# A delta-rule kernel followed by a mixer: the first loads in one queue, betas earlier, the first weight converted in the order of its use, and a new order of all instructions

## The chip, the cores and the metric

The kernel runs on one core of a Trainium2 chip. The metric is device time in microseconds (us), lower is better. A core has five engines that run their own instruction streams in order: TensorE (PE, with its weight loads shown as PEld), VectorE (DVE), ScalarE (ACT), GpSimd (POOL) and SyncE (SP), which here only issues transfers. Transfers move in DMA queues between HBM and the core's SBUF.

## The reference

Two computations stand one behind the other. For batch 4, 8 heads, 768 steps and head size 48:

```python
k_n = k / (norm(k) + 1e-06)
for t in range(S):
    y[t] = q[t] @ state
    v_old = state.T @ k_n[t]
    state = state + beta[t] * outer(k_n[t], v[t] - v_old)
```

The outputs of the 8 heads, side by side, are x (4, 768, 384). Then

```python
h = (x.T @ U @ V)          # over the sequence, rank 32
u = x + h.T
out = u + relu(u @ w_ch1) @ w_ch2    # 384 -> 1536 -> 384
```

U, V, w_ch1 and w_ch2 arrive as float64; all else is float32, and so are the matmuls.

## The kernel before, in words

**Units.** The delta rule is computed in chunks of 64 steps. A unit is one batch and one half of the sequence (6 chunks, all 8 heads), so there are 8 units; units 0 and 1 are batch 0. Two SBUF tiles (slot0, slot1) hold the units in turn, so unit 2 can be loaded when unit 0 is done. For each unit:

- `load` brings k, q, v and z (z is a second copy of half of k for the state update) in pieces of 72 KB. `load_beta` brings the betas and turns them with TensorE (L343), ScalarE (L350) and VectorE (L358).
- `grams` transposes k or q (L408 on PE, copied by L418/L420/L423), then multiplies k by k or k by q (L435). L445 and L448 cut the diagonal blocks out of the k products.
- `blocks` lays these blocks out (L517), scales them with the norms and betas (`norms`, L374 to L388, and L521) and inverts the small triangular blocks by substitution on VectorE (L526, L532, in 15 steps for units 0 and 1). The result is turned back (L539, L548).
- `joins` merges inverted blocks into larger ones with many small matmuls (L582, L596, L622 to L643), and `prepare` multiplies k and v by the inverse (L741, L752).
- `recur` steps over the chunks: b (L790), z on VectorE (L803), the state's update (L818, then L828 or L830 on VectorE), and the output in two parts (L705, L719), copied into X by ScalarE (L689).

**Mixer.** When a batch's 12 chunks are in X, `front` computes X @ U (L969), the correction with V (L983), adds it (L987), and transposes X for the products (L991, L994). `wide` does, for each third of a batch (i = 0, 1, 2): the first product (L1062, 12 blocks f of 128 columns, three matmuls each, ReLU by L1018 in pairs of blocks), then the second product in seven parts (L1099), which saves one multiplication of eight by sums of operands (S1, S2 and sums of w_ch2). A part works on 6 matmuls and is added to X by L1047; finished rows go out.

**Weights.** `load_weights` brings 14 slices of float64 (U, V, six of w_ch1, six of w_ch2) into three staging places (half of X, `wide`, part of `hs`) and rebuilds float32 from the bits: five VectorE instructions (L918, L924, L930, L936, L946) and one on ScalarE (L903) for each slice. Four sums for each half of w_ch2 (L858) follow. A slice of w_ch1 held 128 rows by half of the columns, so the first block of the first product needed three slices.

**What sets the order.** Each of these pieces is a Python generator that yields what it needs (`need(...)`) and what it is about to issue (`op(engine, cost, ...)`). `run` plays them against a model of the engines' clocks and each time issues the instruction that the model finds earliest, with the rank of the piece (second argument of `begin`, low first) as the tie-breaker. The emission order is then the order on every engine and queue, with no runtime choice: the costs, the ranks and the table of constants do nothing on the chip but set this order. TensorE's cost is multiplied by `state["slow"]` (1.9) until the first product starts. `lot`, `words` and `FETCH` model the fetching of TensorE's instructions.

Of the kernel before, what the change touches and what calls it, by code (L numbers as in the profile page):

```python
# [26 lines left out]
def kernel(  # L27
# [33 lines left out]
    NU = 2  # L61
# [23 lines left out]
    state = dict(now=0.0, mode=None, hw=0.0, slow=1.9, lot=63, fetched=0.0)  # L85
    free = dict(pair={x: 0.0 for x in range(4)}, mix={})
    done, parts, waits, ready, last = {}, {}, {}, {}, {}
    LAT = dict(pe=0.22, dve=0.06, act=0.06, pool=0.1, sp=0.0)
    SWITCH, HOLD = 0.18, 0.18
    LOT, FETCH = 256, 3.9  # L90

# [6 lines left out]
    def op(engine, cost, mode=None, take=None, give=(), lat=None, rush=None, words=0, port=None):  # L98
        return dict(
            e=engine, cost=cost, mode=mode, take=take, give=give, words=words + 2,  # L100
            port=engine == "pool" if port is None else port,
            rush=bool(give) if rush is None else rush, lat=LAT[engine] if lat is None else lat,
        )
# [4 lines left out]
    def emitted(key, after=0.0):  # L108
        done[key] = state["now"] + after

    def landing(packets, each=0.015):
        state["hw"] = max(state["hw"], state["now"]) + packets * each / 16
        return max(2.0, state["hw"] + 2.4 - state["now"])

    def advance(i, value, at):
        try:
            waits[i], ready[i] = parts[i].send(value), at
        except StopIteration:
            del waits[i]

    def begin(part, place):
        i = (place, len(parts))
        parts[i], waits[i] = part, []
        advance(i, None, state["now"])
# [5 lines left out]
    def cost_of(s):  # L130
        return s["cost"] * (state["slow"] if s["mode"] else 1.0)

# [8 lines left out]
    def run():  # L141
        stall = {}
        while waits:
            some = {}
            for i in sorted(waits):
                while isinstance(waits.get(i), list) and all(x in done for x in waits[i]):
                    at = max([0.0] + [done[x] for x in waits[i]])
                    if at > ready[i]:
                        last[i] = None
                    advance(i, None, max(at, ready[i]))  # L150
                s = waits.get(i)
                if s is None or isinstance(s, list):
                    continue
# [12 lines left out]
                some.setdefault(e, []).append((at + stall[i], i))  # L166
            if not some:
                continue
            picks = []
            for e, them in some.items():  # L170
                soon = min(at for at, _ in them)
                them.sort(key=lambda x: (not waits[x[1]]["rush"], x[1]))
                for at, i in them:
                    hold = 0.7 if i[0] < 13 else HOLD if i[0] < 90 else SWITCH
# [12 lines left out]
            cost = cost_of(s)  # L187
            if s["e"] == "pe":
                crossed, more = late(s, at)
                state["lot"] += s["words"]  # L190
                if state["lot"] > LOT:
                    state["lot"] -= LOT
                    cost += more
                    state["fetched"] = crossed + more + FETCH
# [79 lines left out]
    w1_sb = const.tile([128, KT, DFF], FP32, name="w1_sb")  # L274
# [9 lines left out]
    SPLIT, QUARTERED = (0, 1), (2,)  # L284

# [8 lines left out]
    def load(n, name, halves):  # L294
# [12 lines left out]
        queue = dict(sp=nc.sync, act=nc.scalar, pool=nc.gpsimd)[e]  # L307
# [17 lines left out]
    def load_beta(u):  # L325
# [10 lines left out]
        for cu in range(UC):  # L336
            c = UC * u + cu
            if cu % 3 == 0:
                got = yield op("pe", 0.4, "Q", take=None if cu else "pair", words=24)
            if cu == 0:  # L340
                x, p_bt = got, one(got)[:, 0 : 4 * B * UC].rearrange("p (c x) -> p c x", c=UC)
            for g in range(2):
                nc.tensor.matmul(  # L343
                    p_bt[half(g), cu], beta_sb[:, g, c * L : c * L + L],
                    ident[0 : 4 * B, 0 : 4 * B], start=True, stop=True,
                )
# [54 lines left out]
    def grams(n, i):  # L401
        kn, kq, pg, qk, qn, _, diag, _ = units[n]

        def turn(t, j, i):
            x = yield op("pe", 0.8, "F", take="pair", words=12)
# [22 lines left out]
        def products(j, i):  # L428
            yield need(("laid", n)) if i else []
            x = yield op("pe", 0.7, "Q", take="pair", words=96)  # L430
# [63 lines left out]
    def blocks(n):  # L494
# [66 lines left out]
        def joins(h):  # L561
# [5 lines left out]
            if split == 2:  # L567
# [6 lines left out]
                for y, e in enumerate(es):  # L574
                    if y % 6 == 0:
                        got = yield op("pe", 0.37, mode, take=None if y else "pair", words=words)
# [12 lines left out]
                for y, e in enumerate(es):  # L589
                    if y % 6 == 0:  # L590
                        got = yield op("pe", 0.37, mode, take=None if y else "pair", words=words)
# [23 lines left out]
            for y, (r, c) in enumerate(spots):  # L615
                if y % 3 == 0:
                    got = yield op("pe", 0.18, "J", take=None if y else "pair", words=48)
# [13 lines left out]
            for y, (r, c) in enumerate(spots):  # L631
                if y % 3 == 0:
                    got = yield op("pe", 0.18, "J", take=None if y else "pair", words=48)
# [43 lines left out]
    def recur(b):  # L677
# [19 lines left out]
        def outputs(c, s_old):  # L697
# [3 lines left out]
            y = yield op("pe", 0.24, "Q", take="pair", words=32)  # L701
            p_y = pair(y)[:, :, 0 : 2 * D]
            if c > 0:
# [11 lines left out]
                yield op("pe", 0.24, "Q", words=32)  # L715
# [16 lines left out]
        def prepare(n, h):  # L732
# [4 lines left out]
            x = yield op("pe", 0.7, "Q", take="pair", words=96)  # L737
# [10 lines left out]
            y = yield op("pe", 0.7, "Q", take="pair", words=96)  # L748
# [27 lines left out]
        for c in range(NC):  # L776
# [9 lines left out]
            else:  # L786
                xb = yield op("pe", 0.24, "Q", take="pair", words=32)
# [24 lines left out]
            if c < NC - 1:  # L812
                yield need(("y1", b, c)) if c else []
                xs = yield op("pe", 0.24, "Q", take="pair", words=32)
# [18 lines left out]
    WIDE = 768  # L833

    def weight_slices():
        yield u_sb.rearrange("p c r -> p (c r)"), moe_U, "c"
        yield v_sb, moe_V, ""
        for f in range(2):
            for t in range(KT):
                rows = slice(t * 128, t * 128 + 128)  # L840
                yield (
                    w1_sb[:, t].rearrange("p (a b x) -> p b a x", a=2, b=2)[:, f],
                    moe_w_ch1[rows].rearrange("p (a b x) -> p b a x", a=2, b=2)[:, f], "a",
                )
# [16 lines left out]
    def load_weights():  # L861
# [14 lines left out]
        def start(i):  # L876
# [9 lines left out]
            elif kind == "a":  # L886
                pieces = [(to.rearrange("p (a x) -> p a x", a=2), src)]
# [12 lines left out]
        def raised(i, power):  # L900
            cost = 0.16 + power.shape[1] * 0.001
# [9 lines left out]
        for i in range(len(slices)):  # L911
# [31 lines left out]
            if len(dst.shape) > 2:  # L943
                dst = dst if len(dst.shape) == 3 else dst.rearrange("p a f d -> p a (f d)")
# [14 lines left out]
    def front(b, i):  # L959
# [20 lines left out]
        def block(c):  # L980
# [7 lines left out]
            o = yield op("pe", 0.56, "F", take="pair", words=6)  # L988
# [20 lines left out]
    def wide(b, i):  # L1009
        yield need(("front", b, i), ("narrow", *before(b, i)))  # L1010
        x, ut = X[:, b % 2], uts[b, i]
        if b == 0 and i == 0:
            yield ["mixing"]
            state["slow"] = 1.0
# [40 lines left out]
        for y, fs in enumerate(((0, 1), (2, 6), (7, 8), (3, 4), (5, 9), (10, 11))):  # L1055
            for f in fs:
                yield need(("weights", 1 + KT * (f // 3 % 2 + 1)))
# [3 lines left out]
                for t in range(KT):  # L1061
                    nc.tensor.matmul(  # L1062
                        p_f[:, fs.index(f)],
                        w1_sb[:, t, f * 128 : (f + 1) * 128],
# [42 lines left out]
    with tc.manual_schedule():  # L1107
        begin(load(0, "k", (0,)), 3)
        begin(load(0, "k", (1,)), 3)
        begin(load_beta(0), 12)  # L1110
# [3 lines left out]
        for n in range(N):  # L1114
# [4 lines left out]
            if n:  # L1119
                begin(load(n, "k", (0, 1)), 20 + 4 * n)  # L1120
            begin(load(n, "q", (0, 1)), 21 + 4 * n)
            begin(load(n, "v", (0, 1)), 22 + 4 * n)
            begin(load(n, "z", (0, 1)), 23 + 4 * n)
# [39 lines left out]
```

## Time and profile before

| | |
|---|---|
| median of 3 runs | 654.01 us (652.53 to 655.49) |
| profiled execution: time, span | 652.64 us, 650.9 us |
| busy: PE, PEld, DVE, ACT, POOL | 600.8, 522.4, 393.6, 228.6, 63.5 us |
| instructions | 23417, of them 10536 matmuls |
| mean granted TensorE clock | 0.926 |

The span is the time from the first to the last instruction; 1.74 us of the profiled execution lie outside it. In the trace each matmul stands twice (L1062 864 times, for 432 in the order below), so an `x8` of the order is `x16` in the trace; transposes (L408, L991) stand once. PE is busy for 92% of the span, but the average hides two different stretches: the first 160 us, with gaps and a halved clock, and the rest, in which it is hardly ever idle.

### The profile page before, as it was taken

The numbers are of one execution on the slowest core, as the hardware profiler recorded it, in microseconds if no ns is written. First come the engines' busy times: TensorE is split into PE (matmuls) and PEld (weight loads), VectorE is DVE, ScalarE is ACT, GpSimd is POOL, SyncE is SP. The second block draws the span as 40 slices with busy tenths as digits, with TensorE's granted clock in tenths as the row PEclk, the third lists the DMA queues.
The fourth block names the chain that finished last, engine by engine and source line by source line (L and its number), as shares of the span: only waits on it lengthen the run. The fifth ranks groups of instructions, "written<-read, shape, count | busy, mean of one in ns | idle before, by whom it ended". The sixth has DMA issues, their size and how long they took to land.

```text
span 650.9 us, 23417 instructions
## 1 busy us (share of the span) xinstructions
PE 600.8 (92%) x10536; PEld 522.4 (80%) x10536; DVE 393.6 (60%) x957; ACT 228.6 (35%) x450; POOL 63.5 (10%) x93
## 2 busy tenths in 40 slices
PE   5479987789999999999999999999999999999997
PEld 4378886467889878697888977897888878999987
DVE  5578766969997824699887228986793123131212
ACT  4344465642033363542524433435124131111020
POOL 7332010000130010010201001011001000000000
PEclk9555555989999999999999999999999999999999
DMA  9910366781000032350000513200000000000000
GB/s 164 164 45 5 115 149 155 144 218 20 25 4 3 28 57 41 60 117 16 4 28 10 107 43 72 54 31 3 2 26 3 27 3 1 24 1 25 12 13 25
DMA packets 89955, 33.26 MB, mean 51 GB/s; under 512 B 81600, under 2 KB 87744, under 8 KB 89856
## 3 DMA queue, kind: packets, MB, share of 16 engines
q1 hardware_dynamic: 86944, 29.41, 20.7%
q0 software_dynamic: 1312, 2.07, 1.6%
q8 instruction: 83, 1.36, 0.8%
q10 hardware_dynamic: 1600, 0.30, 0.2%
q14 instruction: 16, 0.13, 0.1%
HBM read 27.03 MB, written 4.72 MB: 49 GB/s over the span
## 4 chain that ended last, share of the span: by engine, by line
PE 69%; DVE 15%; SPq 4%; DMA 4%; ACT 3%; issue 3%; DVEq 0%; ACTq 0%
PE P L1062 25%; PE P L1099 22%; SPq L312 4%; DVE prod L526 3%; DVE xt L532 3%; PE P L435 3%; PE P L790 2%; DMA slot<-in_k_dram 2%; PE P L582 2%; PE P L705 2%; PE P L752 2%; PE P L983 2%; PE P L408 1%; PE P L596 1%; PE P L719 1%
## 5 line engine op out<-in xcount | busy, mean ns | idle before, releaser
L1062 PE MATMUL P<-ut,w_sb 128*128 128x256 f32 x864 | 202.1, 387 | 0.0
L1062 PEld LDWEIGHTS P<-ut,w_sb 128*128 128x128 f32 x864 | 160.9, 191 | 22.7 <-issue 0.6
L1099 PE MATMUL P<-w_sb,hs 128*128 128x192 f32 x720 | 126.6, 329 | 1.4 <-DVE X L1047 1.3
L1099 PEld LDWEIGHTS P<-w_sb,hs 128*128 128x128 f32 x720 | 116.7, 190 | 3.6 <-DVE X L1047 1.6
L1018 ACT ACTIVATE hs<-P 128x512 f32<-128x512 f32 x72 | 43.0, 597 | 198.3 <-PE P L1062 176.5
L1047 DVE TENSOR_TENSOR X<-X,P 128x192 f32<-128x192 f32 x84 | 29.7, 353 | 78.5 <-PE P L1099 78.0
L532 DVE TENSOR_TENSOR xt<-xt,prod 128x112 f32<-128x112 f32 (+21 forms) x200 | 66.4, 332 | 6.9
L526 DVE TENSOR_TENSOR prod<-gs,xt 128x112 f32<-128x112 f32 (+21 forms) x200 | 65.0, 325 | 4.5
L689 ACT COPY X<-P 64x192 f32<-64x192 f32 x96 | 30.0, 313 | 63.6 <-PE P L719 62.5
L1099 PE MATMUL P<-w_sb,S 128*128 128x192 f32 x288 | 50.8, 330 | 0.0
L408 PE MATMUL P<-ident,slot 128*128 128x128 f32 x192 | 31.9, 316 | 16.9 <-issue 6.2
L1099 PEld LDWEIGHTS P<-w_sb,S 128*128 128x128 f32 x288 | 46.7, 190 | 0.5
L1034 DVE TENSOR_TENSOR S<-hs 128x384 f32<-128x384 f32 x24 | 13.3, 553 | 49.1 <-ACT hs L1018 49.1
L408 PEld LDWEIGHTS P<-ident,slot 128*128 128x128 f32 x192 | 25.2, 161 | 20.9 <-issue 17.1
L803 DVE TENSOR_TENSOR z<-slot,P 128x192 f32<-128x192 f32 x44 | 15.5, 352 | 37.3 <-PE P L790 23.2
L435 PE MATMUL P<-slot 48*64 48x64 f32 x1536 | 33.7, 240 | 3.7 <-ACT slot L423 2.0
L435 PEld LDWEIGHTS P<-slot 48*64 48x64 f32 x1536 | 29.6, 151 | 8.7 <-issue 3.8
L391 POOL TENSOR_TENSOR slot<-slot,norm_rows 128x1152 f32<-128x1152 f32 x8 | 20.4, 2548 | 156.1 <-DVE norm_rows L388 72.0
L661 ACT COPY slot<-zz 32x384 f32<-32x384 f32 x64 | 32.6, 509 | 6.7 <-DVE zz L600 3.9
L423 ACT COPY slot<-P 128x768 f32<-128x768 f32 x30 | 23.5, 800 | 17.9 <-PE P L408 17.6
L828 DVE TENSOR_TENSOR s<-s,P 128x192 f32<-128x192 f32 x40 | 14.0, 350 | 19.3 <-PE P L818 18.8
L790 PE MATMUL P<-s,slot 48*64 48x48 f32 x704 | 22.3, 243 | 3.0 <-DVE power L918 0.9
(118 smaller groups left out, 748.5 us busy)
## 6 DMA issues: line engine op xcount, KB each, us to landing
slot<-in_k_dram SPq DMA_DIRECT2D x84, 72.0 KB, 3.1
slot<-in_q_dram SPq DMA_DIRECT2D x64, 72.0 KB, 3.3
out_dram<-X SPq DMA_DIRECT2D x24, 192.0 KB, 1.8
slot<-in_v_dram SPq DMA_DIRECT2D x48, 72.0 KB, 2.6
X<-in_moe_w_ch_dram SPq DMA_DIRECT2D x6, 384.0 KB, 3.9
wide<-in_moe_w_ch_dram SPq DMA_DIRECT2D x6, 384.0 KB, 5.0
X<-in_moe_w_ch_dram SPq DMA_DIRECT2D x2, 768.0 KB, 7.3
wide<-in_moe_w_ch_dram SPq DMA_DIRECT2D x2, 768.0 KB, 5.1
```

The source lines that it names most:

```text
L312: queue.dma_start(out=t[half(1 - g if name == "z" else g), :, to, 0:D], in_=src[b, 4 * g + s, hf * UC * L : (hf + 1) * UC * L, :].rearrang ...
L408: nc.tensor.transpose(p_t[:, c // 3, c % 3], t[:, c, 2 * j : 2 * j + 2].rearrange("p s d -> p (s d)"), ident,)
L435: nc.tensor.matmul(p_g[half(g ^ (par * i)), par, c], kq[rows, c, j, 0, half(g)], kq[rows, c, j, i, half(g)], start=True, stop=True,)
L526: nc.vector.tensor_tensor(out=prod, in0=gb[:, :, j : j + 1, j + 1 :].to_broadcast([128, split, m, w]), in1=xb[:, :, 0:m, j : j + 1].to_bro ...
L532: nc.vector.tensor_tensor(out=xb[:, :, 0:m, j + 1 :], in0=xb[:, :, 0:m, j + 1 :], in1=prod, op=ALU.subtract,)
L661: nc.scalar.copy(pg[quarter(i), :, at, :, a : a + BK], cut(zc, h)[quarter(i)].rearrange("p r (c j) t -> p r c j t", j=2),)
L689: nc.scalar.copy(x[half(c % 2), c // 2, 4 * D * g : 4 * D * (g + 1)].rearrange("p (j r d) -> p r j d", r=2, d=D), states(p_y)[half(g)],)
L790: nc.tensor.matmul(states(p_b)[half(g ^ par), par, j], kq[half(par, D), cu, j, 0, half(g)], states(s_old)[half(par, D), g, j], start=True, ...
L1018: nc.scalar.activation(hs[:, fs[0] : fs[1] + 1 : fs[1] - fs[0]], p_f, ACTF.Relu)
L1047: nc.vector.tensor_tensor(out=to, in0=to, in1=p, op=ALU.add)
L1062: nc.tensor.matmul(p_f[:, fs.index(f)], w1_sb[:, t, f * 128 : (f + 1) * 128], ut[:, t], start=(t == 0), stop=(t == KT - 1),)
L1099: nc.tensor.matmul(p_o, a[:, f], w2_sb[:, w, f], start=(first and f == 0), stop=(f == HF - 1), skip_group_check=True,)
```

## The change

- The first two units' loads all go to SyncE's queue (v and z of units 0 and 1 were on GpSimd's), in the order k0 (half of it on ScalarE's queue as before), k1, q0, q1, z0, v0, z1, v1, with the V weights behind z1. Before, q0 stood first, then the V weights, then k1.
- `load_beta(0)` gets rank 4 instead of 12, and so comes directly behind k0's transposes.
- A slice of w_ch1 now holds two blocks f of all 384 rows, in the order in which the first product takes the pairs (`PAIRS`); the first product's pair y needs slice 2 + y alone. The tile is laid out in the same way. Such a slice is loaded with two transfers of 384 KB instead of one of 768 KB.
- The order's model is changed: instruction words, TensorE costs and transfer times, a model of TensorE's granted clock in steps of 3.413 us (`pace`), and a table of ranks (`PLACES`) that replaces those of single pieces. These only move instructions.

The core of the diff:

```diff
+    FIRST = dict(k1=11, q0=12, q1=13, z0=14, v0=15, z1=16, v1=17)
-        elif n < NU and name in ("v", "z"):
-            e = "pool"
...
-        begin(load_beta(0), 12)
+        begin(load_beta(0), 4)
...
+            begin(load(n, name, (0, 1)), FIRST.get((name, n), 20 + 4 * n + y))
...
-    w1_sb = const.tile([128, KT, DFF], FP32, name="w1_sb")
+    w1_sb = const.tile([128, FT // 2, KT * 256], FP32, name="w1_sb")
...
+    PAIRS = ((0, 1), (2, 6), (7, 8), (3, 4), (5, 9), (10, 11))
-        for f in range(2):
-            for t in range(KT):
+        for y, (f, g) in enumerate(PAIRS):
+            of = slice(f, g + 1, g - f)
...
-                yield need(("weights", 1 + KT * (f // 3 % 2 + 1)))
+            yield need(("weights", 2 + y))
...
+    PLACES = """
+    add_up b0 i0 60.5; add_up b1 i0 12.835; block b0 i1 c2 87.0; block b0 i1 c3 87.0
...
+        place = float(PLACES.get(name_of(part), place))
```

Three places of the order. First SyncE's queue at the start. Slots 0 and 1 hold units 0 and 1; the second load of k into a slot is z. Before:

```order
L312 DMA slot0_87<-in_k_dram 64x6x48 x4
L312 DMA slot0_87<-in_q_dram 64x6x48 x8
L896 DMA wide_132<-in_moe_V_dram 32x1536 x4
L312 DMA slot1_88<-in_k_dram 64x6x48 x7
L896 DMA X_129<-in_moe_w_ch1_dram 128x2x768
L312 DMA slot1_88<-in_k_dram 64x6x48
L312 DMA slot1_88<-in_q_dram 64x6x48 x8
```

And now (L367 is the line that was L312, L952 was L896):

```order
L367 DMA slot0_87<-in_k_dram 64x6x48 x4
L367 DMA slot1_88<-in_k_dram 64x6x48 x8
L367 DMA slot0_87<-in_q_dram 64x6x48 x8
L367 DMA slot1_88<-in_q_dram 64x6x48 x8
L367 DMA slot0_87<-in_k_dram 64x6x48 x4
L367 DMA slot0_87<-in_v_dram 64x6x48 x8
L367 DMA slot1_88<-in_k_dram 64x6x48 x4
L952 DMA wide_132<-in_moe_V_dram 32x1536 x4
L367 DMA slot1_88<-in_v_dram 64x6x48 x8
L952 DMA X_129<-in_moe_w_ch1_dram 128x3x256 x2
```

Unit 1's k moves ahead of unit 0's q, the V weights move from the third place behind the z loads, and the loads that GpSimd issued are now in this queue.

Second, VectorE between unit 0's diagonal blocks and the norms. Before:

```order
L517 STREAM_TRANSPOSE gs_115<-slot0_87 128x1024
L930 SCALAR_TENSOR_TENSOR X_129<-X_129 128x192
L936 SCALAR_TENSOR_TENSOR power_133<-X_129,power_133 128x192
L946 SCALAR_TENSOR_TENSOR u_sb_123<-X_129,power_133 128x192
L918 TENSOR_SCALAR power_133<-wide_132 128x768
L466 TENSOR_TENSOR slot0_87<-P_75,mask_u_84 128x6x64 x2
L358 STREAM_TRANSPOSE betas_119<-beta_rows_120 128x128
L377 TENSOR_SCALAR norm_277<-norm_277 128x32
```

And now (L413 was L358, L503 was L448, L572 was L517, L432 was L377, L974 to L1002 were L918 to L946):

```order
L413 STREAM_TRANSPOSE betas_119<-beta_rows_120 128x128
L503 SCALAR_TENSOR_TENSOR slot0_87<-P_75,even_102,slot0_87 128x6x32 x2
L974 TENSOR_SCALAR power_133<-X_129 128x192
L980 TENSOR_SCALAR X_129<-X_129 128x192
L503 SCALAR_TENSOR_TENSOR slot0_87<-P_75,even_102,slot0_87 128x6x32 x2
L572 STREAM_TRANSPOSE gs_115<-slot0_87 128x1024
L986 SCALAR_TENSOR_TENSOR X_129<-X_129 128x192
L992 SCALAR_TENSOR_TENSOR power_133<-X_129,power_133 128x192
L1002 SCALAR_TENSOR_TENSOR u_sb_123<-X_129,power_133 128x192
L432 TENSOR_SCALAR norm_302<-norm_302 128x32
```

The betas are turned ahead of everything that the substitution needs, and the first instruction on the V weights (L918 on `wide`) no longer stands ahead of the norms.

Third, TensorE at the last batch's front. Before (L969 is X @ U, L983 the correction with V, L991 the transposes, L1062 and L1099 the first and second product):

```order
L969 MATMUL P_75<-X_129,u_sb_123 32x384 x6
L1062 MATMUL P_75<-ut_6215,w1_sb_122 128x256 x3
L983 MATMUL P_75<-tt_7170,v_sb_124 128x384 x2
L991 MATMUL P_75<-ident_76,X_129 128x128 x6
L1062 MATMUL P_75<-ut_6215,w1_sb_122 128x256 x6
L983 MATMUL P_75<-tt_7170,v_sb_124 128x384 x2
L991 MATMUL P_75<-ident_76,X_129 128x128 x6
L1099 MATMUL P_75<-w2_sb_125,hs_126 128x192 x12
```

And now (L1025, L1039, L1047, L1117, L1154 in the same sequence of roles):

```order
L1025 MATMUL P_75<-X_129,u_sb_123 32x384 x6
L1117 MATMUL P_75<-ut_6492,w1_sb_122 128x256 x3
L1039 MATMUL P_75<-tt_7183,v_sb_124 128x384 x2
L1154 MATMUL P_75<-w2_sb_125,hs_126 128x192 x6
L1047 MATMUL P_75<-ident_76,X_129 128x128 x6
L1154 MATMUL P_75<-w2_sb_125,hs_126 128x192 x6
L1039 MATMUL P_75<-tt_7183,v_sb_124 128x384 x2
L1154 MATMUL P_75<-w2_sb_125,S2_128 128x192 x6
L1047 MATMUL P_75<-ident_76,X_129 128x128 x6
```

Between the correction and the transposes that wait for VectorE's addition there now stands a part of the second product. In the whole program each of the mixed stretches changes in this way: behind the first second-product part on S2, the large matmuls (L408, L983, L991, L1062, L1099) stood in 85 runs separated by other work, and now stand in 75. Up to that part the program issues the same matmuls as before, except that 2 of L983 and 12 of L991 come after it instead of before.

More of the change, by code (lines that the diff above doesn't have):

```diff
@@ L109, in emitted, with landing @@
         done[key] = state["now"] + after
-    def landing(packets, each=0.015):
-        state["hw"] = max(state["hw"], state["now"]) + packets * each / 16
-        return max(2.0, state["hw"] + 2.4 - state["now"])
+        for i in awaited.pop(key, ()):
+            missing[i].discard(key)
+            if not missing[i]:
+                woken.append(i)
+    def landing(packets, each=0.0235):
+        state["hw"] = max(state["hw"], state["now"] + 1.0) + packets * each / 16
+        return state["hw"] + 0.4 - state["now"]
@@ L115, in advance @@
     def advance(i, value, at):
         try:
-            waits[i], ready[i] = parts[i].send(value), at
+            s, ready[i] = parts[i].send(value), at
         except StopIteration:
-            del waits[i]
+            waits.pop(i, None)
+            return
+        if isinstance(s, list):
+            waits.pop(i, None)
+            asked[i], missing[i] = s, {key for key in s if key not in done}
+            for key in missing[i]:
+                awaited.setdefault(key, []).append(i)
+            if not missing[i]:
+                woken.append(i)
+        else:
+            waits[i] = s
@@ L131, in cost_of, with pace @@
         return s["cost"] * (state["slow"] if s["mode"] else 1.0)
+    def pace(at, end, flow):
+        while int((end - PHASE) / SPAN) > state["span"]:
+            state["span"] += 1
+            edge = PHASE + SPAN * state["span"]
+            part = flow * min(1.0, max(0.0, (edge - at) / max(end - at, 1e-9)))
+            used, flow, at = state["flow"] + part, flow - part, max(at, edge)
+            if used > 0.36 * SPAN or "mixing" in done:
+                state["slow"] = 1.0
+            elif used < 0.28 * SPAN and "mixing" not in done:
+                state["slow"] = 1.9
+            state["flow"] = 0.0
+        state["flow"] += flow
     def late(s, at):
@@ L142, in run @@
         stall = {}
-        while waits:
-            some = {}
[L145 to L153, printed above, removed]
+        while waits or woken:
+            while woken:
+                i = woken.pop(0)
+                at = max([0.0] + [done[x] for x in asked[i]])
+                if at > ready[i]:
+                    last[i] = None
+                advance(i, None, max(at, ready[i]))
+            some = {}
+            for i, s in waits.items():
                 e, was = s["e"], last.get(i)
@@ L886, in start @@
             elif kind == "a":
[L887 removed]
+                to = to.rearrange("p (t f x) -> p t f x", t=KT, f=2)
+                pieces = [(to[:, :, f], src[:, :, f]) for f in range(2)]
             elif kind == "f":
@@ L900, in raised @@
         def raised(i, power):
-            cost = 0.16 + power.shape[1] * 0.001
+            cost = 0.16 + size(i) * 0.001
             yield op("act", cost)
```

95 lines of the change are left out of this document (57 added, 38 removed).

## The prediction

> **What bounds the kernel now.** I first read the page's slices, then the busy time of four stretches (start, length, busy time of PE, PEld, DVE, ACT, POOL, granted clock, share of the DMA engines, GB/s). Three events cut them: A at 40.20, the first matmul of unit 0's joins (L582); B at 69.63, the same for unit 1; C at 161.55, the first part of the second product on S2 (L1099).
>
> ```profile
> PE   5479987789999999999999999999999999999997
> ...
> PEclk9555555989999999999999999999999999999999
> ```
>
> ```profile
> 0.00:40.20 40.20, 21.06 (x384) 17.92 (x384) 25.42 (x83) 18.16 (x33) 20.43 (x37) 0.73 0.85 142
> 40.20:69.63 29.43, 27.05 (x816) 25.58 (x817) 22.68 (x59) 13.22 (x29) 7.37 (x10) 0.50 0.06 16
> 69.63:161.55 91.92, 76.88 (x1627) 66.78 (x1628) 70.17 (x116) 46.85 (x86) 3.65 (x7) 0.76 0.59 142
> 161.55:647.50 485.95, 475.82 (x7711) 412.10 (x7710) 275.09 (x702) 150.34 (x303) 32.05 (x39) 1.00 0.13 29
> ```
>
> Behind C TensorE works for 98% of the time at full clock: there only less work or fewer joints between kinds of work can help. Before A it idles for 19.1 us of 40.2. From A to B it is the bound, at half clock. From B to C it idles 15.0 us, and VectorE, which rebuilds the weights there, 21.7 us. Up to C the program issues the same matmuls as before but for a few; so what reaches C earlier ends earlier, microsecond for microsecond, as long as TensorE stays as full behind C. The sum therefore has four terms: up to A, A to B, B to C, and the rest.
>
> Next I read the chain of waits up to A (start, length, what):
>
> ```profile
> 9.25 6.37 DMA wide<-in_moe_V_dram
> 15.63 7.99 DMA slot<-in_k_dram
> 23.62 1.86 issue
> 25.48 1.53 PE P L408 x6
> ...
> 38.15 2.00 DVE zz L539
> ...
> 67.47 2.12 DVE zz L539
> ```
>
> Unit 1's k waits in the queue behind the V weights and lands at 23.62; the substitution of unit 0 is stalled by unit 1's products, which stand inside it in VectorE's order. VectorE's timeline shows both stalls:
>
> ```profile
> 13.32 1.97 DVE L517 STREAM_TRANSPOSE gs<-slot 128x1024 f32<-128x1024 f32 x1
> ...
> 19.96 0.81 DVE L918 TENSOR_SCALAR power<-wide 128x768 int32<-128x768 int32 x1 [3.77 <-DMA wide<-in_moe_V_dram]
> ...
> 21.62 0.29 DVE L358 STREAM_TRANSPOSE betas<-beta_rows 128x128 f32<-128x128 f32 x1
> ...
> 23.14 0.65 DVE L521 TENSOR_TENSOR gs<-gs,cp 128x512 f32<-128x512 f32 x1
> ...
> 30.12 0.74 DVE L448 SCALAR_TENSOR_TENSOR slot<-P,even,slot 128x192 f32<-128x192 f32 x2 [3.00 <-ACT slot L445]
> ```
>
> **Term 1, up to A: -7.9 us.** The substitution's 30 instructions, grouped between 23.5 and 38.2:
>
> ```profile
> L532 DVE TENSOR_TENSOR xt<-xt,prod 128x30 f32<-128x30 f32 (+7 forms) x15 | 3.8, 254 | 0.5
> L526 DVE TENSOR_TENSOR prod<-gs,xt 128x30 f32<-128x30 f32 (+7 forms) x15 | 3.8, 253 | 0.4
> ```
>
> With their gaps they take 8.6 us, but 14.3 passed. TensorE's betas, the queue's timeline, and the transfers' median times to landing in the first 40 us:
>
> ```profile
> 11.79 0.87 PE L343 MATMUL P<-ident,X 16*64 16x16 f32 x24
> ```
>
> ```profile
> 3.88 5.33 SPq L312 DMA_DIRECT2D slot<-in_q_dram  x8
> ...
> 11.46 8.21 SPq L312 DMA_DIRECT2D slot<-in_k_dram  x7
> ```
>
> ```profile
> slot<-in_q_dram SPq DMA_DIRECT2D x16, 72.0 KB, 5.0
> ...
> X<-in_beta_dram POOLq DMA_DIRECT2D x2, 48.0 KB, 4.1
> ```
>
> Eight loads need 5.33 us of issuing where the queue is not held up. k1 moves to q0's place and is issued by 9.2; it lands by 12 to 14 (3 to 5 us). q0 is issued by 14.5 and lands by 19.5 at the latest, q1 by 24.5. The betas cost TensorE 0.9 us ahead of the k products; issued no later than before, they land by 9 and hold nothing. So the blocks of unit 0 are laid out (L517, now ending at 15.3) about 0.9 us later, at 16.2; the norms, behind the copies of k1 on ScalarE, are done at 18.6; L448's first pair (0.74) and L521 (0.65) end at 20.1. The second pair for unit 1 comes after three steps and waits for q0's transposes, which stand before it on TensorE: 23.2. Twelve steps (7.1) and the turn back (2.0) end at 32.3, against 40.15. The 24 loads of v and z that GpSimd issued now stand in this queue at 0.66 each: unit 0's v is issued by 27.5, the last by 37.5, and `prepare` reads v only behind the joins, after 32 plus their 10 us. These hide them; without that cover each late microsecond would count. Bounds: if the betas, q0 and TensorE's fetching hold each step up by what the page shows for the same step now (1.86 of issue, 3 of landing), only 3 us are gained; with no wait at the second pair, 10.
>
> On the one queue, the Trainium skill (DMA: Bandwidth & Descriptors, Issuing engines are not separate DMA queues) says that transfers from several engines run on the same 16 DMA engines and that spreading them saves issue time only. The trace agrees: the DMA engines are 0.85 busy in this stretch with three queues at work. By that rule the merging costs only issue time, which is the 0.66 used above.
>
> **Term 2, A to B: -3.9 us (29.4 to 25.5).** Of the recursion's groups of eight matmuls, six fewer stand between A and B. One takes about 0.45 us at half clock:
>
> ```profile
> 99.09 0.64 PE L719 MATMUL P<-z,slot 64*64 64x48 f32 x16
> 99.51 0.64 PE L705 MATMUL P<-s,slot 48*64 48x48 f32 x16
> ```
>
> That is 2.7 off 27.05, and 1.2 of 2.4 us of idle time goes with the VectorE waits on the recursion inside unit 1's substitution. Bounds: 0, and -5.
>
> **Term 3, B to C: -4.5 us (91.9 to 87.4).** The six groups come here (+2.7), the two L983 and twelve L991 leave (-2.9, worked out below). So TensorE's 76.9 us stay, and the idle 15.0 us decide. The waits in this stretch (us in total, times, longest):
>
> ```profile
> PE P L408 <- DMA slot<-in_q_dram: 3.2, 1, 3.2
> ...
> DVE S L1034 <- ACT hs L1018: 3.3, 1, 3.3
> ...
> DVE power L918 <- DMA wide<-in_moe_w_ch_dram: 2.8, 1, 2.8
> ...
> PE P L752 <- issue: 2.2, 1, 2.2
> ```
>
> The first and third are the queue's: unit 3's last two q loads and a weight slice stand behind v loads, and now all of unit 3's q stands directly behind one weight slice. With the first goes the half-clock stretch that follows it:
>
> ```profile
> 110.00:111.00 1.00, 1.00 (x39) 0.73 (x40) 0.96 (x2) 0.62 (x1) 0.00 (x0) 0.67 0.06 16
> 141.00:142.00 1.00, 1.00 (x7) 1.00 (x8) 0.97 (x3) 0.00 (x0) 0.00 (x0) 0.69 0.76 107
> 144.00:145.00 1.00, 1.00 (x4) 0.83 (x3) 0.00 (x0) 0.00 (x0) 0.00 (x0) 0.60 1.10 261
> ```
>
> The clock comes up at 110.7, falls at 141.4 and is back at 144.6; 3.3 us at half clock cost 1.6. Together 4.8 on TensorE, and VectorE has 6.1 less to wait. Against that, VectorE's list up to C is 1.5 us longer (the V slice is begun later), and TensorE's fetch waits stay. I take 4.5. Bounds: 0 (a wait of the same size elsewhere), and -10 (two thirds of the idle time).
>
> **Term 4, the rest: -1.5 us.** A run of large matmuls pays at each joint (the chain's pieces, and two neighbours at a front):
>
> ```profile
> 340.94 9.26 PE P L1062 x42
> ...
> 376.26 1.49 PE P L1062 x6
> ...
> 541.20 1.29 PE P L983 x4
> 543.69 13.65 PE P L1099 x84
> ```
>
> ```profile
> 391.23 0.45 PE L705 MATMUL P<-s,slot 48*64 48x48 f32 x16 [0.24 <-DVE z L803]
> ```
>
> ```profile
> L991 PEld LDWEIGHTS P<-ident,X x72: 137/140/143, 121.6 to 575.0; 128*128 128x128 f32 x72
> ```
>
> Six L1062 alone cost 1.49, in a long run 9.26 / 7 = 1.32: 0.17, and about as much again for the entry of the small groups; 10 fewer runs, -3.3. With fewer runs between, the recursion's groups follow one another directly in 12 steps where 4 did, at 0.24 each: +1.9. At a front, four L983 and six L991 need 1.29 + 6 x 0.14 = 2.13, but 2.49 pass; eight such neighbours are now parted by other work: -3. The work that moved here is 2 x 0.65 + 12 x 0.14 = +2.9. Bounds: +5 (the joints save nothing) and -6 (half of the 10.1 us idle goes as well).
>
> **Sum.** -7.9 - 3.9 - 4.5 - 1.5 = -17.8 against the profiled execution's 652.64 (span 650.9 and 1.74 around it): 634.8. The median of the runs is 1.4 above that execution, so I predict 636.
>
> Hidden edits: the new shape of the w_ch1 slices makes the first product wait for one slice instead of three, but L1062 starts long after the last of these slices is rebuilt:
>
> ```profile
> 116.19 0.96 DVE L946 SCALAR_TENSOR_TENSOR w_sb<-X,power 128x768 f32<-128x768 f32 x1
> ```
>
> ```profile
> 130.87 5.35 PE L1062 MATMUL P<-ut,w_sb 128*128 128x256 f32 x24
> ```
>
> So this alone is worth nothing now; if the start moves by more than 14 us, it begins to count. Two transfers for one cost SP 0.6 us each in a queue that is not waited for there.
>
> **Rivals.**
>
> R1, the clock rises early: the work that is pressed together between A and B could bring the clock up there. For it: nothing but density. Against it: this stretch is 92% busy at 0.50 now, and the same kinds of matmuls fill it. If it came, B would fall another 9 us (half of 25.5 less one stretch of 3.4 at half clock), and the time would be 627. The Trainium skill (TensorE: Matmul & The Clock Gate, Part 1) lets the clock up after one busy window of about 3.4 us; by that rule R1 would hold, and before would already have shown it, which the trace contradicts.
>
> R2, the start gains little: TensorE's own fetch and the q0 transposes ahead of unit 1's second products hold the substitution as k1 does now. For it: VectorE would wait at the same instruction. Term 1 is then -3, the time 641; with terms 2 and 3 at their poor ends as well, 648.
>
> R3, no change: VectorE, which must rebuild eleven slices and more between B and C at up to 4.8 us each (five instructions of at most the 0.96 above), is the true bound up to C, and TensorE waits for it at the second product. VectorE's 70.2 us of 91.9 speak against it; it needs C to stay at 161, so 650 to 654.
>
> R4, slower, by the clock alone: it is granted from 110.7 on, after the transposes of unit 2. If TensorE's work there gets gaps as long as the 3.2 us before 141, the stretch that ran at full clock up to C would run at half in part.
>
> ```profile
> 110.67:161.55 50.88, 41.19 (x587) 33.28 (x582) 42.97 (x68) 24.56 (x41) 0.00 (x0) 0.97 0.57 131
> ```
>
> That is 41 us of work. Each 10 us of that work costs 10; from 18 us on the kernel is slower, about 660 if 25 are hit. The waits that went are against it. The Trainium skill (same page, same part) says that an idle window of about 3.4 us halves the clock; the fall at 141.4 after 3.2 idle us agrees.
>
> **Chances.** My sum 0.62 (628 to 645), R1 0.10, R2 0.17 (half of it at 645 to 650), R3 0.05, R4 0.06. The range 626 to 648 leaves out R3, R4 and the poorest part of R2. A change within 0.5% (3.3 us) cannot be told from none: faster 0.89, same 0.05, slower 0.06.
>
> **What would show it.** Up to A: the betas' transpose before 12, no wait on the V weights ahead of the norms, the turn back of unit 0 ending near 32 and of unit 1 near 58. B to C: no long wait for unit 3's q, no fall of the clock between its rise and C, C near 145. Behind C: TensorE's idle time under 10 us and the stretch no longer than 486. Wrong would be: A after 37 (R2), a clock that rises before B (R1) or falls again (R4), or C near 161 with VectorE full (R3).

## The result, and the profile after

The changed kernel takes 628.45 us (median of four runs, 627.76 to 629.01) against 653.58 for the kernel before (652.53 to 655.49): the ratio is 0.9612, with a 95% interval of 0.9586 to 0.9638. The forecast was 636. The profiled execution took 629.01 us, with a span of 627.2.

Lines moved by the diff: L408 of before is now L463, L582 is L637, L991 is L1047, L1099 is L1154, L539 is L594, and the recursion's L705, L719, L790, L803, L818 and L830 are L760, L774, L845, L858, L873 and L885.

First the page's slices for TensorE and its clock, and the four stretches between the same events as before (A 32.05, B 58.30, C 143.90; columns as before):

```profile
PE   5598879899989999999999999999999999999997
...
PEclk9855557999989999999999999999999999999999
```

```profile
0.00:32.05 32.05, 17.20 (x384) 15.15 (x385) 22.62 (x77) 16.77 (x32) 5.08 (x16) 0.92 0.69 115
32.05:58.30 26.25, 24.41 (x721) 22.98 (x721) 21.49 (x60) 13.15 (x27) 6.80 (x7) 0.50 0.43 94
58.30:143.90 85.60, 74.52 (x1707) 65.06 (x1707) 73.84 (x120) 44.42 (x81) 3.86 (x7) 0.77 0.60 152
143.90:623.80 479.90, 472.92 (x7730) 416.07 (x7726) 275.52 (x702) 153.07 (x310) 31.59 (x39) 1.00 0.13 29
```

Up to A 8.15 us went, from A to B 3.2, from B to C 6.3, and behind C 6.05 (to the span's end). VectorE's timeline shows the start as forecast: the betas' turn before 12, the norms at 18.1 with no V slice ahead of them, the second pair for unit 1 without a wait, and the turns back that end at 31.9 (the last line) and 58.2:

```profile
11.46 0.31 DVE L413 STREAM_TRANSPOSE betas<-beta_rows 128x128 f32<-128x128 f32 x1 [1.18 <-ACT beta_rows L405]
...
18.09 0.17 DVE L432 TENSOR_SCALAR norm<-norm 128x32 f32<-128x32 f32 x1
...
22.14 0.73 DVE L503 SCALAR_TENSOR_TENSOR slot<-P,even,slot 128x192 f32<-128x192 f32 x2
...
29.96 1.95 DVE L594 STREAM_TRANSPOSE zz<-xt 128x1024 f32<-128x1024 f32 x1
```

Behind C, TensorE works 2.9 us less and idles 7.0 us instead of 10.1. Its waits there (us in total, times, longest), before, first the matmuls', then the weight loads':

```profile
PE P L991 <- DVE X L987: 1.8, 2, 1.4
PE P L1099 <- DVE X L1047: 1.3, 1, 1.3
PE P L719 <- DVE z L803: 1.0, 4, 0.3
PE P L790 <- DVE s L830: 0.9, 2, 0.6
```

```profile
PEld P L991 <- DVE X L987: 8.6, 15, 2.0
```

And now, the longest (one of the joins') first:

```profile
PE P L677 <- DVE zz L655: 1.4, 1, 1.4
...
PE P L774 <- DVE z L858: 0.5, 2, 0.2
...
PE P L1154 <- DVE X L1102: 0.4, 1, 0.4
PE P L1047 <- DVE X L1043: 0.4, 1, 0.4
```

```profile
PEld P L873 <- DVE z L858: 2.2, 11, 0.2
...
PEld P L1047 <- DVE X L1043: 0.9, 2, 0.8
```

The recursion's steps wait about as often as forecast (13 times), but eleven of these waits are listed at the weight load, while an earlier matmul still runs for most of the time: of their 2.2 us TensorE idles 0.9, in gaps of some 0.08 us that are too short for the list of the matmuls. In the same way TensorE idled only 2.8 of the 8.6 us that are listed above.

### The profile page after: what moved, and what is told of

The parts are those of the page before. It is cut to its first block, busy times and chain, and to the rows that moved or that the text cites. A ratio compares the mean times of both kernels' runs of the same rounds, so it can differ in the third digit from the quotient of the medians.

```text
span 627.2 us, 23410 instructions
## 1 busy us (share of the span) xinstructions
PE 589.1 (94%) x10536; PEld 519.3 (83%) x10536; DVE 393.7 (63%) x957; ACT 227.4 (36%) x450; POOL 47.3 (8%) x69
## 3 DMA queue, kind: packets, MB, share of 16 engines
q1 hardware_dynamic: 99712, 31.18, 22.1%
## 4 chain that ended last, share of the span: by engine, by line
PE 72%; DVE 20%; issue 3%; ACT 2%; DMA 1%; SPq 1%; DVEq 0%; ACTq 0%
PE P L1154 24%; PE P L1117 23%; DVE xt L587 5%; DVE prod L581 5%; PE P L490 3%; PE P L796 2%; PE P L463 2%; PE P L845 2%; PE P L1039 2%; PE P L807 2%; PE P L873 2%; PE P L637 2%; DVE zz L594 2%; PE P L651 2%; PE P L760 1%
## 5 line engine op out<-in xcount | busy, mean ns | idle before, releaser
L1117 PE MATMUL P<-ut,w_sb 128*128 128x256 f32 x864 | 202.1, 387 | 0.6 <-ACT ut L1050 0.6
L1117 PEld LDWEIGHTS P<-ut,w_sb 128*128 128x128 f32 x864 | 161.4, 192 | 24.4 <-issue 1.2
L1154 PE MATMUL P<-w_sb,hs 128*128 128x192 f32 x720 | 125.9, 329 | 0.4 <-DVE X L1102 0.4
L1154 PEld LDWEIGHTS P<-w_sb,hs 128*128 128x128 f32 x720 | 117.2, 190 | 3.5 <-DVE X L1102 0.7
L587 DVE TENSOR_TENSOR xt<-xt,prod 128x112 f32<-128x112 f32 (+21 forms) x200 | 64.6, 323 | 6.9
L1089 DVE TENSOR_TENSOR S<-hs 128x384 f32<-128x384 f32 x24 | 16.7, 694 | 63.3 <-ACT hs L1073 63.3
L1154 PE MATMUL P<-w_sb,S 128*128 128x192 f32 x288 | 51.1, 330 | 0.0
L1154 PEld LDWEIGHTS P<-w_sb,S 128*128 128x128 f32 x288 | 46.7, 190 | 1.1
L463 PE MATMUL P<-ident,slot 128*128 128x128 f32 x192 | 29.4, 304 | 10.9 <-POOL xt L566 5.1
L858 DVE TENSOR_TENSOR z<-slot,P 128x192 f32<-128x192 f32 x44 | 15.5, 353 | 37.7 <-PE P L845 27.8
L463 PEld LDWEIGHTS P<-ident,slot 128*128 128x128 f32 x192 | 24.3, 156 | 14.2 <-POOL xt L566 5.1
L490 PEld LDWEIGHTS P<-slot 48*64 48x64 f32 x1536 | 27.2, 145 | 5.2 <-ACT slot L478 2.4
L490 PE MATMUL P<-slot 48*64 48x64 f32 x1536 | 30.3, 232 | 0.9 <-ACT slot L478 0.7
L1050 ACT COPY ut<-P 128x384 f32<-128x384 f32 x24 | 10.6, 479 | 42.8 <-PE P L1047 33.3
```

The costliest lines, as they stand in the source:

```text
L463: nc.tensor.transpose(p_t[:, c // 3, c % 3], t[:, c, 2 * j : 2 * j + 2].rearrange("p s d -> p (s d)"), ident,)
L490: nc.tensor.matmul(p_g[half(g ^ (par * i)), par, c], kq[rows, c, j, 0, half(g)], kq[rows, c, j, i, half(g)], start=True, stop=True,)
L587: nc.vector.tensor_tensor(out=xb[:, :, 0:m, j + 1 :], in0=xb[:, :, 0:m, j + 1 :], in1=prod, op=ALU.subtract,)
L1117: nc.tensor.matmul(p_f[:, fs.index(f)], w1_sb[:, y, 256 * t + 128 * fs.index(f) :][:, 0:128], ut[:, t], start=(t == 0), stop=(t == KT - 1),)
L1154: nc.tensor.matmul(p_o, a[:, f], w2_sb[:, w, f], start=(first and f == 0), stop=(f == HF - 1), skip_group_check=True,)
```

## The experiments

Each time is the median of its runs; its ratio is to the kernel before on the same chip. Pieces of TensorE's order keep their places unless the text says otherwise. Stretches of the profiled executions, in us:

```
run                          A     A-B    B-C   behind C  ratio (95%)
before                     40.20  29.43  91.92  489.35    1
changed                    32.05  26.25  85.60  483.30    0.9612 (0.9586-0.9638)
e9  changed, once more     32.42  25.74  87.50  482.54    0.9623 (0.9592-0.9654)
e12 no ranks               32.42  28.18  85.00  487.80    0.9755 (0.9723-0.9787)
e1  no ranks behind C      31.77  27.60  83.11  511.92    1.0053 (1.0024-1.0082)
e11 old loads, new order   40.32  25.88  84.56  482.84    0.9721 (0.9690-0.9751)
e4  old order, k1 first    42.88  29.33  91.52  490.07    1.0039 (1.0005-1.0072)
e2  q0 ahead of k1         37.40  25.88  84.72  483.60    0.9624 (0.9580-0.9669)
e3  3.9 us ahead of A      36.16  25.87  83.77  482.10    0.9683 (0.9640-0.9726)
e7  old w_ch1 slices       32.04  25.93  84.34  483.09    0.9604 (0.9566-0.9642)
e8  v and z on GpSimd      32.60  25.93  83.91  482.36    0.9606 (0.9567-0.9644)
e10 transposes ahead of A  32.31  27.10  83.74  482.75    0.9655 (0.9615-0.9696)
```

The unchanged kernel's second profile differs from its first by 1.9 us between B and C, so differences of that size in one profile decide nothing.

**Loads and order: e11 and e4.** In e11 the order on the compute engines is the changed kernel's, the loads are issued as before (a sketch of the queues, not the code):

```diff
 SP:     k0 x4
-        k1 x8, q0 x8, q1 x8, z0 x4, v0 x8, z1 x4, V x4, v1 x8
+        q0 x8, V x4, k1 x8, q1 x8
 GpSimd: (behind U)
+        z0 x4, v0 x8, z1 x4, v1 x8
```

> The changed kernel's order on every engine with the kernel before's order of loads: unit 0's q and the four V weight loads ahead of unit 1's k, v and z of the first units issued by GpSimd. Theory: order and loads are one edit. Unit 1's k lands at 22 to 24, its copies stand ahead of unit 0's norms on ScalarE, so the norms come at 26 to 27 instead of 18.1: A at 39 to 42, the time 635 to 639. Rival: only the order on the engines counts: A below 36, the time within 2 of the unchanged kernel's.

635.3 us, 6.5 above e9, with A back at 40.32, as the theory had it. The longest wait of VectorE up to A names the step:

```profile
DVE norm L447 <- ACT norm L444: 5.9, 1, 5.9
```

ScalarE takes the norms' root (L444 here) only behind its copies of unit 1's k. e4 comes from the other side: the kernel before, with k1's loads alone moved ahead of q0's.

> The kernel before with one thing alone: unit 1's eight k loads are issued ahead of unit 0's q loads and the V weights; every engine's order stays that of before. Theory: unit 1's k no longer lands at 23.6; but on TensorE unit 0's q transposes and products still stand ahead of it and VectorE's V weight slice and the late betas still stand ahead of unit 0's norms, so only the 3.0 us wait inside the substitution goes: A at 36 to 38 instead of 40.2, the time 648 to 651. Rival: the load order is the whole of term 1: A at 32 to 33, the time about 645.

655.1 us, against 652.4 for the kernel before beside it, and A came at 42.88, later than before. Both theories missed. VectorE's timeline (lines of that kernel):

```profile
24.18 0.78 DVE L925 TENSOR_SCALAR power<-wide 128x768 int32<-128x768 int32 x1 [7.43 <-DMA wide<-in_moe_V_dram]
...
26.03 0.13 DVE L384 TENSOR_SCALAR norm<-norm 128x32 f32<-128x32 f32 x1
```

The wait changed its place: the V weights now land last, and in the old order their slice stands ahead of the norms. Before, that wait was 3.77. So neither the new order alone nor k1's move alone reaches A at 32; together with the rest of the loads they do. The whole new queue under the old order, with the V weights later still, was not tried, nor was the betas' place alone.

**One move undone: e2** (again a sketch of the queue).

```diff
 SP: k0 x4
-    k1 x8, q0 x8
+    q0 x8, k1 x8
```

> The changed kernel with one move undone: unit 0's eight q loads are issued ahead of unit 1's eight k loads; every engine's order is otherwise the changed kernel's. Theory (term 1): unit 1's k lands about 4.5 us later, its copies stand ahead of unit 0's norms on ScalarE, so the norms and the substitution start 3 to 4 us later: A at 35 to 36.5 instead of 32.05, and the end moves as far: 631.5 to 633. Rival: unit 1's products are hidden behind VectorE's own list, A moves by less than 1 us and the time stays within 1 of 628.5.

A moved by 5.35, even more than expected, and the profiled execution took 633.3. But that was the slowest of four; the others took 626.1 to 629.3. The median, 629.2, is the rival's time, and the interval reaches only the low end of the theory's. A's shift is shown, its price is not.

**A delay of known size: e3.**

```diff
-        nc.vector.transpose(zz..., xt...)
+        for _ in range(3 if n == 0 else 1): nc.vector.transpose(zz..., xt...)
```

> The changed kernel with the turn back of unit 0 written three times (same input, same output): 3.9 us more on VectorE directly ahead of A, nothing else. Theory (microsecond for microsecond): A at 35.95, B and C as much later, the stretch behind C unchanged, the time 632.4 (631.5 to 633.5). Rival: waits further on (VectorE's for weight slices, TensorE's between B and C) take it up: the time rises by less than 2 us, C by less than 2.

A at 36.16; 631.6 us, and the ratio is 0.0060 above e9's, 3.9 us, though the two intervals overlap. In the profiled execution C came 1.9 later than in the first profile of the changed kernel, and 0.1 later than in the second. The median speaks for microsecond for microsecond, not closer than some 3.5 us. Against e9's A at 32.42, then, shifts of 7.9 (e11), 3.7 (e3) and 5.0 us (e2) cost 6.5, 3.9 and 0.1: that a microsecond at A is one at the end fits the first two, and e2 leaves it open.

**The ranks: e12 and e1.** e12 empties the table of places; e1 takes out only the twenty entries whose pieces act behind C.

> The changed kernel with an empty table of searched ranks: the new loads, the betas first, the pairs of w_ch1 and the order model's new costs stay. Theory: up to A the loads and the betas' place do the work (A at 31.5 to 33.5); behind it the ranks do, since without those behind C a whole substitution stood uncovered: C at 145 to 152, the stretch behind C 500 to 515, the time 648 to 665. Rival: that hole came from half a table, and the model without any ranks gives a whole order: the stretch behind C 484 to 490, the time 632 to 640.

638.0 us, 9.2 above e9. A is the same: up to there the loads, the betas' place and the model's new costs do the work, as e12 keeps all three. Behind C the stretch is 5.3 longer than in e9, and e9's row is the second one here:

```profile
145.60:630.00 484.40, 475.66 (x7718) 415.89 (x7716) 271.91 (x693) 150.83 (x305) 31.25 (x39) 1.00 0.14 30
```

```profile
145.66:624.80 479.14, 472.89 (x7732) 415.83 (x7726) 275.42 (x702) 153.34 (x311) 31.17 (x39) 1.00 0.13 29
```

2.8 of it is TensorE's work, 2.5 idle time. In the count of runs of large matmuls behind C, 85 before and 75 now, e12 has 84. Without ranks TensorE waits there for two things that the ranks take away in the main (the second was 0.5 in 2 above):

```profile
PE P L463 <- DMA slot<-in_q_dram: 2.2, 1, 2.2
PE P L774 <- DVE z L858: 1.8, 6, 0.4
```

The rest of the 9.2 is harder to place: e12 reaches C at 145.6, e9 at 145.7, and e1, e7, e8, e10 and the first profile, with the ranks up to there, at 142.3 to 143.9.

The rival was right on the time (632 to 640) and on the stretch behind C (484 to 490): 489.35 to 487.80 without ranks, and 5.3 more with them.

> The changed kernel without the twenty searched ranks of pieces that act behind C (units 5 to 7, sequences 1 to 3); the order is the same on every engine up to C and beyond, and differs only later. Theory: the stretch behind C came out 6 us shorter instead of the forecast 1.5 because the ranks part the neighbours at the fronts, so that the transposes there no longer wait for VectorE's sums (8.6 us in 15 waits before, 0.4 in one after). Without the late ranks these waits come back in part: C stays at 143.9, the stretch behind it grows from 483 to 486 to 490, the time is 631 to 635. Rival: the model's corrected costs alone give that order, the late ranks are decoration: C at 143.9 and the time within 1.5 of 628.5.

656.7 us: all of the gain lost. The stretch behind C grew by 28.6, and most of it is one wait:

```profile
PE P L845 <- DVE slot L521: 20.0, 1, 20.0
```

From 261 to 281 VectorE is at a later unit's substitution and its turns back, with nothing on TensorE beside it. e12, without any rank, has no such hole. Both theories missed, and half of a searched table is not half of its gain. On the fronts, for which e1 was meant, its trace speaks against the theory: the transposes there (L1047) wait 0.4 us in one place, as in the changed kernel, so the late ranks did not take these waits away.

**Hidden edits: e7 and e8.** e7 puts the halves of w_ch1 back (one transfer a slice, three slices for the first pair), e8 the 24 loads of v and z on GpSimd.

```diff
-    w1_sb = const.tile([128, FT // 2, KT * 256], FP32, name="w1_sb")
+    w1_sb = const.tile([128, KT, DFF], FP32, name="w1_sb")
```

```diff
-        queue = dict(sp=nc.sync, act=nc.scalar)[e]
+        queue = nc.gpsimd if n < NU and name in ("v", "z") else dict(...)[e]
```

> The changed kernel with the layout of w_ch1 undone alone: the slices hold half the rows of 768 columns again, with one transfer each, and the first product's first pair needs three of them; the order is the changed kernel's. Theory (hidden edit): the last of the six slices is rebuilt at 103.7, the first product starts at 114.9, so nothing waits for it: time 628.5, within 1.5. Rival: the pairs free the start of the first product: without them C and the end come 2 us or more later (over 630.5).

> The changed kernel with one move undone: the 24 loads of v and z of units 0 and 1 are issued by GpSimd again; the orders are otherwise the changed kernel's. Theory (hidden edit): these loads are read only behind the joins, and the 16 DMA engines are shared whoever issues; A within 1 of 32.05, time within 1.5 of 628.5. Rival: issued early, they compete with unit 0's and 1's k and q: those land 2 to 5 us later, A moves by as much, the time is 630 to 633.

627.4 and 627.8 us (ratios 0.9604 and 0.9606, each within 0.004): both worth nothing, as expected. In e8 A came at 32.60, with the DMA engines 0.91 busy up to there instead of 0.69.

**The clock: e5, e6 and e10.** These add transposes of the identity that nobody reads: 34 ahead of A and one or two ahead of each piece from A to B (e5), the same on up to unit 2's transposes (e6), or 22 ahead of A alone (e10).

```diff
+    heat = lambda n: [nc.tensor.transpose(P[:, 0, 384:512], ident, ident) for _ in range(HEAT.get(n, 0))]
```

> The changed kernel with 71 transposes of the identity added on TensorE that nobody reads: 34 in its idle stretch ahead of A, and one or two ahead of each piece of work between A and B. Nothing else moves. Theory (R1's mechanism, the clock follows how much dense work TensorE has, not how busy it is): the granted clock stays near full from 28 through B instead of 0.50; VectorE, 21.5 us busy of 26.25 there, becomes the bound; A stays at 32 to 32.5, the stretch A to B falls from 26.25 to 22 to 23.5, the time to 624 to 626. Rival: the clock falls anyway (small matmuls, with or without the added work, count as idle), the added transposes cost 0.28 each in a stretch that TensorE bounds: A to B rises to 34 to 37, the time to 635 to 640.

> As the run before, with the added transposes carried on through the recursion up to unit 2's transposes (some 130 more). Theory: the clock stays near full to C; TensorE's 26 us of work at half clock between B and 100 shrink, and VectorE, busy 73.8 of 85.6 between B and C, takes over as the bound: C at 132 to 138 instead of 143.9, the time 616 to 624. Rival: VectorE and the weight slices' loads bound this stretch already: C no earlier than in the run before, the time 624 to 628.

> The changed kernel with 22 transposes of the identity that nobody reads, on TensorE in its idle stretch ahead of A only (the run with 71 lost its time between A and B, where the added work stood in TensorE's way and the clock fell all the same). Theory: the clock is granted in stretches of 3.4 us by the dense work of the stretch before; so one stretch behind A runs at full clock, A stays at 32 to 32.5, A to B falls by 1 to 2, the time is 1 to 2 below the unchanged kernel's of this call. Rival: the chain through VectorE and ScalarE takes the gain up, or the transposes themselves run at half clock and reach past A: no difference, or up to 1.5 slower.

e5 took 636.6 us (ratio 0.9731, 0.9687 to 0.9775), the rival's time; A to B grew to 33.7. Three stretches from about the end of the 34 transposes on:

```profile
32.16:35.57 3.41, 3.41 (x71) 2.84 (x69) 1.66 (x4) 1.82 (x5) 2.98 (x2) 1.00 0.83 184
35.57:38.98 3.41, 3.41 (x60) 2.66 (x57) 3.39 (x6) 0.90 (x3) 0.06 (x1) 0.77 1.08 195
38.98:52.64 13.66, 13.66 (x269) 10.79 (x272) 5.88 (x19) 4.65 (x10) 2.94 (x3) 0.50 0.33 85
```

The clock is up to 37.4, then half again although TensorE never idles: about one added transpose a microsecond does not hold it. A denser dose was not tried. e6 took 658.5 (1.0044, 1.0010 to 1.0078), slower than both theories, with B to C at 102.9; its output is wrong, so only its time is read. e10 took 630.2, no gain on e9's 628.8, as its rival had it: A at 32.31 with the clock full up to there, and A to B 27.1 at 0.59. No version here beats the changed kernel by more than the runs differ.

## Why the forecast was near, and where it missed

The sum's four terms came out at -23.7 instead of -17.8. R1's time, 627, is nearer to the measured 628.45 than the forecast 636; that is luck, because the clock behind A stayed at 0.50 in the first profile.

**Term 1** (-7.9, measured -8.15): right in size and in its chain from the loads to the norms, but two steps of it were wrong and cancel. Unit 0's q landed at 21.9 and 23.4 (the two halves) and not by 19.5, and TensorE multiplies unit 1's k ahead of q's transposes, not behind them. So the second pair did not need q and came at 22.1 instead of 23.2:

```profile
19.30 1.63 PE L490 MATMUL P<-slot 48*64 48x64 f32 x96
21.86 0.85 PE L463 MATMUL P<-ident,slot 128*128 128x128 f32 x6 [0.93 <-DMA slot<-in_q_dram]
```

e11 and e4 add what the sum did not say: the new order gains nothing up to A without the new loads, and k1's move nothing without the new order.

**Term 2** (-3.9, measured -3.2 and, in e9, -3.7): in the first profile the six recursion groups, -2.6 of work as forecast, and -0.5 of idle time instead of -1.2. Without the ranks it is -1.25 (e12), and TensorE runs 814 matmuls there, against 816 before and 721 now: the ranks move the groups.

**Term 3** (-4.5, measured -6.3 and, in e9, -4.4): no long wait for unit 3's q is left, and C is at 143.9 and 145.7, near the forecast 145. The term was still too small: in the six other profiles with the changed kernel's order from B to C and no added work there (e2, e3, e7, e8, e10, e11) the stretch took 83.7 to 84.7, so -7.2 to -8.2. Of the 6.3 here 4.0 is idle time and 2.4 is work, which the sum left as it was. (By its row, 0.60 from 144 to 145, the clock before was back at 144.8 and not at 144.6; that changes the term by 0.1.) One sign was wrong: the clock did fall once between its first rise and C.

```profile
76.50:83.40 6.90, 5.03 (x175) 4.69 (x173) 6.50 (x14) 2.58 (x5) 0.00 (x0) 0.75 0.49 157
83.40:100.50 17.10, 13.23 (x425) 12.35 (x425) 13.18 (x22) 9.56 (x20) 2.05 (x4) 0.50 0.67 164
100.50:143.90 43.40, 39.41 (x643) 31.98 (x641) 38.14 (x60) 21.18 (x36) 0.00 (x0) 0.99 0.63 143
```

The fall that R4 feared came, but from a rise that before did not have, and at 81.2, where TensorE had idled for only 1.0 of the last 3.4 us and not for the 3.2 in one piece that R4 weighed. From 100.5 on the clock stays up, 10 us earlier than before; that is where the work shrinks.

**Term 4** (-1.5, measured -6.05 and, in e9, -6.8) is the term that was mis-sized. Its work came out: -2.9 by the busy time, against -3.4 in the sum (-3.3, -3 and +2.9; the -3 was read from elapsed time, so some of it is idle time). What one joint costs was not isolated: e12, with 84 runs, works 475.66 against 475.82 before, but eight more transposes stand behind C there.

The step that failed is the +1.9 for exposed recursion waits: idle time was to grow and fell by 3.15. Twelve steps at 0.24 were charged to TensorE. It idles 1.7 us ahead of all the recursion's matmuls (L760, L774, L845, L873) where it idled 4.5, so -2.8 instead of +1.9, above all because the 2.0 ahead of L790, most of it waits for the state's update, are gone. Ahead of the fronts' transposes and the second product it idles 0.8 instead of 4.1. Against that, it idles 3.4 ahead of the joins instead of 0.5.

e12 divides this. Without ranks the fronts' waits are as good as gone too (0.1), so they are not the ranks' doing, but that of what e12 keeps, the model's new costs above all (argued: this was not tried alone). The recursion's waits are at 3.3 without ranks and 1.7 with them. That e12's stretch is 1.55 shorter than before, about the -1.5 forecast, is a coincidence: 0.16 of it is work and 1.4 idle time, where the sum had less work and more idle time. Which rank does how much was not tried.

The terms leave 5.9 of the 7.6 us between forecast and median; the other 1.9 is the step from one execution to the median, +1.4 in the forecast and -0.56 in fact, with 0.1 the other way outside the span.

**R1** had the wrong price. (Its own sum gives 11 rather than 9: half of 25.5, less the 1.7 that one stretch of 3.4 forgoes.) In e9 the clock was up in part from A to B, with the same program:

```profile
32.42:58.16 25.74, 21.74 (x720) 20.80 (x720) 22.91 (x60) 13.67 (x28) 6.70 (x7) 0.63 0.44 95
```

TensorE's busy time fell by 2.7 and the stretch by 0.5: TensorE now waits 3.1 us in one piece for VectorE's update of the state (L885), where it waited 0.7, and VectorE is busy for 22.9 of the 25.7 us. The 9 us were half of TensorE's time, with no look at the engine behind it. On the rule weighed there (the Trainium skill, TensorE: Matmul & The Clock Gate, Part 1), the trace disagrees again: in the first 13.41 us behind A TensorE is busy for all 13.41 at 0.50.

```profile
32.05:45.46 13.41, 13.41 (x340) 13.13 (x342) 9.82 (x25) 7.07 (x15) 3.37 (x3) 0.50 0.79 170
```

**R2 and R3** are out: A at 32.05, and C 18 us earlier with VectorE 73.8 busy of 85.6.

## What to carry to other kernels

A transfer that was moved ahead paid here only with the engines' orders moved too; moved alone, the wait came back at what the old order put next (7.4 us). Charge TensorE with its own idle time, not with what its weight loads wait: 8.6 us listed at the weight loads were 2.8 of idle time, and 2.2 were 0.9. Before an engine's time is halved in a sum, look how long the next engine is busy in the same stretch.

## What the runs showed of the hardware

Being busy was not enough for TensorE's full clock: it was at half for 13.66 of 13.66 us busy with small matmuls and some 13 transposes between them (e5), and it fell to half there behind 3.41 us without any idle time. The kind of work alone did not decide either: one and the same program had 0.50 and 0.63 from A to B in two executions, and in e9 the clock rose at 48.6 among the same small matmuls. What decides was not found. Single executions of one kernel lay up to 10 us apart (e4, 649.8 to 659.9).
